# First product of the last expert layer: seven block products in place of eight

## The chip, the cores and the metric

The kernel runs on one core of a Trainium2 chip. A core has TensorE (PE in the profile; PEld is its weight load), VectorE (DVE), ScalarE (ACT), GpSimd (POOL), and SyncE (SP), which issues most transfers. The metric is the device time of one execution in microseconds (us), as the median of several.

## What is computed

```python
x = attn_out.reshape(B * S, D)          # spectral mixing of (4, 3072, 256)
x = _moe_ref(x=x, **moe_kwargs)         # top-1 experts, 384 slots each
...
logits = x @ w_gate                     # last expert layer
P = np.exp(logits - logits.max())
for _ in range(8):                      # Sinkhorn: rows, columns
    ...
for e in range(E):                      # E = 8, D = 256, F = 1024
    h = np.maximum(x @ w1[e], 0.0)
    ye = h @ w2[e]
    out += P[:, e:e + 1] * ye
```

The last layer works on all tokens with every expert. The kernel does it for the 8 x 384 = 3072 slots of the first expert layer; the other rows of the output are zero.

## The kernel before

Every float32 operand of a large product is split into a high part, rounded to what a float32r matmul takes, and a low part, the rest. A product of two such operands is three matmuls that add up in one PSUM bank: high by high, low by high and high by low.

The first expert layer (lines 714 to 739) goes through 8 experts, two halves of the 1024 hidden columns, and four 128-wide tiles each: `mm1` (675) fills a ps_h bank with 6 matmuls of 384 columns, ACT writes the Relu as the high part (682), DVE the low part (683), and `mm2_a` (697), two tiles later, adds it into two ps_yT banks. At an expert's end ACT and DVE write those banks to `x_hi` and `x_lo` (708, 709), the input of the last layer, and `logits2` (685) makes the gate's logits from them, 4 small matmuls for each of 24 tiles of 128 tokens.

The last layer (863 to 910) has blocks of one expert, one half and 512 of the 3072 tokens. For a block PE runs `mm1` for four hidden tiles (24 matmuls of 512 columns, line 680), and then the second product of the block before, `mm2_b` (822): 24 matmuls into two ps_y banks (834). DVE multiplies each bank by the row weights `pb` (843) and adds it to `acc` (844); for expert 1 POOL first multiplies `acc` by expert 0's weights (826). The last expert takes both halves of a block one after the other, its last 512 tokens in two blocks of 256, and `finish` (846) transposes finished tokens and sends each row to its place by an indirect transfer (857).

The order on each engine is the order of the code (`manual_schedule`). PE's products are one block ahead of its second products, so a block's Relus have a whole block's time. The weights of a half come by SP one half ahead (`load_w`, 414, two 512 KB transfers) and are split by ACT and POOL (`split_w`, 426) in four pieces of 512 columns, at blocks 1 to 4 of the half before; three weight sets, w0 to w2, take turns. The Sinkhorn steps (`sink`, 800) are put between the matmuls of the first blocks, each with one small matmul on PE and ten small operations on DVE. ps_h has 3 banks, ps_y and ps_yT share 4.

## Time and profile before

| what | before |
|---|---|
| runs | 1506.34, 1508.4 and 1510.44 us; median 1508.4 |
| the profiled execution's own time | 1509.36 us |
| its span, first to last instruction | 1507.6 us |
| busy in the span | PE 1467.9 (97%), DVE 819.1 (54%), ACT 489.2 (32%), POOL 291.4 (19%) |
| mean granted PE clock | 0.987 |

The page divides the span by engine and by line. A busy PE is not a PE at its peak, since matmuls overlap; the spacing of their starts tells how fast they run. "<-" in a group stands between output and inputs; "idle before" is the time that the engine stood before the group's instructions, with what ended it. The table of stretches gives each engine's busy time within a window, and the granted clock as a share of 2.4 GHz.

### The profile page before, as it was taken

How to read it: one execution, taken by the hardware profiler on the slowest of the kernel's cores; microseconds unless marked ns; L12 is line 12 of the kernel's file. 1: busy time of each engine (PE TensorE's matmuls, PEld its weight loads, DVE VectorE, ACT ScalarE, POOL GpSimd, SP SyncE). 2: the span in 40 equal slices, each digit the busy share in tenths (PEclk: the TensorE clock that was granted, in tenths of full speed). 3: DMA queues.
4: the chain of work that ended last, by engine and by line, in shares of the span. 5: the costliest groups of instructions: out<-in, count | busy, mean ns of one | idle time of the engine just before them, and what ended most of it. 6: DMA issues, size and time to landing. Idle time of an engine off the chain costs nothing.

```text
span 1507.6 us, 19030 instructions
## 1 busy us (share of the span) xinstructions
PE 1467.9 (97%) x7372; PEld 1240.0 (82%) x7372; DVE 819.1 (54%) x1456; ACT 489.2 (32%) x944; POOL 291.4 (19%) x349
## 2 busy tenths in 40 slices
PE   8999897799999999999999999999999999999997
PEld 7988786799988888888888888888888888888887
DVE  4768688465557235545445455455544554454444
ACT  3444565355533222222222222222222222222222
POOL 2344355712211002210100101010000101020222
PEclk9999998899999999999999999999999999999999
DMA  9447771633320411422201010111101011101111
GB/s 243 110 130 177 189 198 45 192 112 112 112 85 1 156 43 56 156 75 91 75 31 57 22 50 28 49 36 42 54 24 49 29 49 28 50 22 28 49 42 37
DMA packets 70601, 118.07 MB, mean 78 GB/s; under 512 B 7334, under 2 KB 41478, under 8 KB 69062
## 3 DMA queue, kind: packets, MB, share of 16 engines
q1 hardware_dynamic: 55078, 94.79, 21.0%
q0 software_dynamic: 14656, 21.71, 5.5%
q8 instruction: 59, 0.97, 0.3%
q10 hardware_dynamic: 768, 0.28, 0.1%
q14 instruction: 40, 0.33, 0.1%
HBM read 88.34 MB, written 28.41 MB: 77 GB/s over the span
## 4 chain that ended last, share of the span: by engine, by line
issue 65%; PE 9%; POOL 6%; DMA 1%; another core or an unknown queue 0%; POOLq 0%; ACT 0%; DVE 0%; SPq 0%; ACTq 0%
POOL w L87 5%; PE ps_h L680 4%; PE ps_yT L704 4%; POOL out_dram L857 1%; POOL acc L826 1%; DMA raw<-in_moe_w_dram 1%; PE lg L689 0%; PE ps_t L668 0%; DMA xg<-xs_d,idx 0%; DMA pb<-p_d 0%; POOLq L87 0%; POOLq L1015 0%; ACT w L86 0%; POOLq L857 0%
## 5 line engine op out<-in xcount | busy, mean ns | idle before, releaser
L682 ACT ACTIVATE hh<-ps_h 128x512 fp32r<-128x512 f32 (+2 forms) x456 | 263.2, 577 | 841.0 <-PE ps_h L680 823.6
L834 PE MATMUL ps_y<-hh,w 128*128 128x512 f32 (+1 forms) x1568 | 499.9, 391 | 0.0
L680 PE MATMUL ps_h<-x_hi,w 128*128 128x512 f32 (+1 forms) x1568 | 493.1, 386 | 0.0
L683 DVE SCALAR_TENSOR_TENSOR hl<-ps_h,hh 128x512 fp32r<-128x512 f32 (+2 forms) x456 | 302.1, 663 | 319.9 <-ACT hh L682 312.6
L834 PEld LDWEIGHTS ps_y<-hh,w 128*128 128x128 f32 x1568 | 292.3, 188 | 66.7
L680 PEld LDWEIGHTS ps_h<-x_hi,w 128*128 128x128 f32 x1568 | 292.6, 188 | 60.2
L834 PE MATMUL ps_y<-hl,w 128*128 128x512 f32 (+1 forms) x784 | 305.6, 390 | 0.0
L680 PE MATMUL ps_h<-x_lo,w 128*128 128x512 f32 (+1 forms) x784 | 302.2, 385 | 0.0
L87 POOL TENSOR_TENSOR w<-raw,w 128x512 fp32r<-128x512 f32 x84 | 109.5, 1305 | 930.6 <-ACT w L86 853.1
L843 DVE TENSOR_TENSOR yp<-ps_y,pb 128x512 f32<-128x512 f32 (+1 forms) x172 | 117.0, 680 | 237.4 <-PE ps_y L834 231.0
L834 PEld LDWEIGHTS ps_y<-hl,w 128*128 128x128 f32 x784 | 147.2, 188 | 33.7
L680 PEld LDWEIGHTS ps_h<-x_lo,w 128*128 128x128 f32 x784 | 147.3, 188 | 29.7
L844 DVE TENSOR_TENSOR acc<-acc,yp 128x512 f32<-128x512 f32 (+1 forms) x172 | 121.6, 707 | 7.4 <-POOL acc L826 1.1
L704 PE MATMUL ps_yT<-hh,w 128*128 128x384 f32 x256 | 77.1, 343 | 4.6 <-issue 2.4
L680 PE MATMUL ps_h<-xgh,w 128*128 128x384 f32 x256 | 78.9, 351 | 0.1
L86 ACT CAST w<-raw 128x512 fp32r<-128x512 f32 x124 | 75.6, 614 | 0.0
L704 PEld LDWEIGHTS ps_yT<-hh,w 128*128 128x128 f32 x256 | 48.2, 191 | 5.3 <-issue 2.8
L680 PEld LDWEIGHTS ps_h<-xgh,w 128*128 128x128 f32 x256 | 48.8, 194 | 0.9 <-ACT xgh L86 0.5
L87 DVE TENSOR_TENSOR ml<-ps_m,mh 128x512 fp32r<-128x512 f32 x48 | 33.2, 692 | 27.7 <-ACT mh L86 27.6
L857 POOL DMA_INDIRECT out_dram<-o,ido x24 | 23.5, 980 | 126.7 <-ACT o L854 121.5
L86 ACT CAST mh<-ps_m 128x512 fp32r<-128x512 f32 x48 | 28.2, 587 | 58.6 <-PE ps_m L158 58.6
L680 PE MATMUL ps_h<-xgl,w 128*128 128x384 f32 x128 | 44.1, 345 | 0.5 <-issue 0.5
(183 smaller groups left out, 1360.0 us busy)
## 6 DMA issues: line engine op xcount, KB each, us to landing
raw<-in_moe_w_dram SPq DMA_DIRECT2D x60, 512.0 KB, 5.4
pb<-p_d SPq DMA_DIRECT2D x88, 256.0 KB, 3.3
out_dram<-zt SPq DMA_DIRECT2D x24, 512.0 KB, 5.4
mf<-in_c_mats_dram POOLq DMA_DIRECT2D x40, 192.0 KB
ds<-d SPq DMA_DIRECT2D x48, 128.0 KB, 3.4
xc<-ds SPq DMA_DIRECT2D x8, 768.0 KB, 6.3
xs_d<-xo SPq DMA_DIRECT2D x32, 192.0 KB, 4.0
xc<-in_x_dram SPq DMA_DIRECT2D x7, 768.0 KB, 13.7
```

The source lines that it names most:

```text
L86: nc.scalar.copy(hi_ap, src)
L87: (lo_engine or nc.vector).tensor_sub(lo_ap, src, hi_ap.bitcast(F32))
L680: nc.tensor.matmul(ps[:, 0:n], l, r[:, h, cols], start=k == 0, stop=k == 5)
L682: nc.scalar.activation(hh, ps[:, 0:n], AF.Relu)
L683: nc.vector.scalar_tensor_tensor(hl, ps[:, 0:n], 0.0, hh.bitcast(F32), op0=ALU.max, op1=ALU.subtract)
L704: nc.tensor.matmul(yT[e][c], l, r, start=fk == 0 and i == 0, stop=fk == 2 * NF - 1 and i == 2)
L826: nc.gpsimd.tensor_mul(acc[:, c, cs], acc[:, c, cs], p0[:, 0:n])
L834: nc.tensor.matmul(ps[:, 0:n], l, r, start=i == 0, stop=i == 3 * NF - 1)
L843: nc.vector.tensor_mul(y[:, 0:n], ps[:, 0:n], pb[:, 0:n])
L844: nc.vector.tensor_add(a, a, y[:, 0:n])
L857: i = nc.gpsimd.indirect_dma_start(out=out, out_offset=bass.IndirectOffsetOnAxis(ap=ido[:, ti % NCH, ti // NCH:ti // NCH + 1], axis=0), in ...
```

## The change

The first product x @ w1[e] is done by Strassen's scheme (in Winograd's form): both operands are cut into two by two blocks, and seven block products stand for eight. On the weight side the blocks are the two 128-row halves of the depth by a pair of 128-wide hidden tiles; on the token side the two depth halves by two token sets, the slots of the even experts of the first layer and those of the odd ones (1536 each). The sums of token blocks, T1 to T4, are made once, at the end of each pair of experts in the first layer (`keep_y`, and two tasks in `later`), and split like x itself. The sums of weight blocks, four 128 by 128 ones for each quarter of the hidden columns, are made by POOL after each load (`sums`), and split by ACT and POOL (`split_r`: 1408 columns a quarter in place of 1024, weights of the second product included).

A unit is one expert, one half, 512 columns of a token set (so 1024 tokens) and one pair of hidden tiles (fp = 0 or 1). It has seven steps. In step i PE runs product i (3 matmuls into a ps_h bank) and 3 or 4 of the 24 second products of the unit before. `post` then makes the four sums of products in the tiles cc: seven additions of a bank and a kept tile on DVE, one copy on ACT, four Relus into the high parts and two in place on ACT, and the low parts, two on POOL and two on DVE. Four ps_y banks (two output halves by two token sets) gather both units of a pair (fp = 0, 1); in the second unit after a pair's start, steps 5 and 6 and the two steps behind them, DVE multiplies each by the row weights and POOL, in the last half DVE, adds it to acc (`evict`). The weight set of the next even quarter is split in a half's third unit, us[2], that of the odd one in the first unit of the next half. hh2 and hl2 of the first layer have 3 buffers in place of 4; the row weights come in one transfer for both token sets; constants move to a pool that ends earlier. The second product's matmuls stay as many. `mm2_b` and the block loop go.

```diff
+    Q = S // 2
+    b_hi = xpl.tile([128, 4, Q], F32R, tag="z1h", name="b_hi")
+    b_lo = xpl.tile([128, 4, Q], F32R, tag="z1l", name="b_lo")
+    t_x = xp.tile([128, 5, Q], F32R, name="t_x")
+    xh = [b_hi[:, i] for i in range(4)] + [t_x[:, i] for i in range(3)]
+    xl = [b_lo[:, i] for i in range(4)] + [t_x[:, 3], t_x[:, 4], wt[0][:, 4608:4608 + Q]]
+    B11, B21, B22, T4, T1, T2, T3 = range(7)
...
+        m, side = divmod(e, 2)
+        terms = ((0, (T1, B11)), (1, (B22,))) if side else ((0, (B11,)), (1, (B21,)))
+        mm = [(h, a[i], w) for h, ops in terms for i in ops for a, w in ((xl, E), (xh, 2 * E))]
...
+    def keep_y(e, y0, y1):
+        m, side = divmod(e, 2)
+        q = slice(cap * m, cap * m + cap)
+        f0, f1 = (xg[:, e].rearrange("p c d -> p (c d)")[:, cap * k:cap * k + cap] for k in range(2))
+        if side == 0:
+            for i, y, f in ((B11, y0, f0), (B21, y1, f1)):
+                split(xh[i][:, q], xl[i][:, q], y)
+                nc.scalar.copy(f, y)
+            return
+        p0, p1_ = (xg[:, e - 1].rearrange("p c d -> p (c d)")[:, cap * k:cap * k + cap] for k in range(2))
+        nc.scalar.copy(f1, y1)
+        nc.vector.tensor_sub(f0, y0, p0)
+        nc.vector.tensor_sub(p0, f1, y0)
+        split(xh[B22][:, q], xl[B22][:, q], y1)
+        nc.gpsimd.tensor_sub(f1, f1, f0)
+        nc.gpsimd.tensor_sub(p1_, p1_, f1)
+        later.append(lambda: (split(xh[T1][:, q], xl[T1][:, q], f0), split(xh[T2][:, q], xl[T2][:, q], f1, nc.gpsimd)))
+        later.append(lambda: (split(xh[T3][:, q], xl[T3][:, q], p0, nc.gpsimd),
+                              split(xh[T4][:, q], xl[T4][:, q], p1_, nc.gpsimd)))
...
-            cs = slice(cap * e, cap * e + cap)
-            for c in range(2):
-                nc.scalar.copy(x_hi[:, c, cs], yT[e][c])
-                nc.vector.tensor_sub(x_lo[:, c, cs], yT[e][c], x_hi[:, c, cs].bitcast(F32))
-            del yT[e]
+            keep_y(e, *yT.pop(e))
...
+    def sums(t, u):
+        a11, a21, a12, a22 = (t[:, 128 * i:128 * i + 128] for i in range(4))
+        s1_, s2_, s3_, s4_ = (u[:, 128 * i:128 * i + 128] for i in range(4))
+        nc.gpsimd.tensor_add(s1_, a21, a22)
+        nc.gpsimd.tensor_sub(s3_, a11, a21)
+        nc.gpsimd.tensor_sub(s2_, s1_, a11)
+        nc.gpsimd.tensor_sub(s4_, a12, s2_)
+
+    WN = 1408
+
+    def split_r(r, t, u, part):
+        w = wt[(1 + r) % 3]
+        for src, o in ((t[:, 0:128], 0), (t[:, 256:512], 128)) if part == 0 else ((u, 384),) if part == 1 else ((t[:, 512:1024], 896),):
+            n = src.shape[1]
+            split(w[:, o:o + n], w[:, WN + o:WN + o + n], src, nc.gpsimd)
...
+    spare = [hp.tile([128, BL], F32R, name=f"h{i}") for i in range(5)]
+    spare += [wt[i][:, o:o + BL] for i, o in ((1, 2816), (1, 3328), (2, 2816), (2, 3328), (0, 2816), (0, 3328), (0, 3840))]
+    pairs = [(spare[2 * i], spare[2 * i + 1]) for i in range(6)]
+    full = [(BL * k, BL) for k in range(Q // BL)]
+    ends = full[:-1] + [(Q - BL, BL // 2), (Q - BL // 2, BL // 2)]
+    units = [(e, h, c0, n, fp) for e in range(E) for h in range(2)
+             for c0, n in (ends if (e, h) == (E - 1, 1) else full) for fp in range(2)]
+    NU2, NS = len(units), 7
...
+    def evict(e, h, c0, n, c, side, ps, last):
+        a = acc[:, c, side, c0:c0 + n]
+        if e == 0 and h == 0:
+            nc.scalar.copy(a, ps[:, 0:n])
+            return
+        y = hp.tile([128, BL], F32, tag="py", name="yp", bufs=2)
+        if e == 0:
+            nc.vector.tensor_add(y[:, 0:n], ps[:, 0:n], a)
+            nc.gpsimd.tensor_mul(a, y[:, 0:n], pbs[0, c0][:, side, 0:n])
+        else:
+            nc.vector.tensor_mul(y[:, 0:n], ps[:, 0:n], pbs[e, c0][:, side, 0:n])
+            (nc.vector if last else nc.gpsimd).tensor_add(a, a, y[:, 0:n])
...
+        seq = [((1, 1), (0, 1), (0, 0), (1, 0)), ((0, 0), (1, 1), (0, 1), (1, 0))][fp]
...
+    PRODS = ((0, B11), (4, T2), (1, B21), (5, T3), (3, T1), (6, B22), (2, T4))
+    MM2 = (3, 4, 3, 4, 3, 4, 3)
...
+            at(us[2], 0, lambda r=r: sums_r(r))
+            for k in range(3):
+                at(us[2], 2 + k, lambda r=r, k=k: split_r(r, rws[r], sus[r], k))
+        r += 1
+        if r < 4 * E:
+            at(us[3], 0, lambda r=r: begin_r(r))
+            at(us[5], 1, lambda r=r: sums_r(r))
+            for k in range(3):
+                at(us[5] + 1, k, lambda r=r, k=k: split_r(r, rws[r], sus[r], k))
...
+    def post(u, i, ps, cc, n, hs):
+        def tile_c():
+            return hp.tile([128, BL], F32, tag="cc", name="cc", bufs=5)
+
+        def high(k, f, side):
+            nonlocal npair
+            hs[f, side] = pairs[npair % 6]
+            npair += 1
+            nc.scalar.activation(hs[f, side][0][:, 0:n], cc[k][:, 0:n], AF.Relu)
+            if k in (0, 3):
+                nc.scalar.activation(cc[k][:, 0:n], cc[k][:, 0:n], AF.Relu)
+
+        def low(k, f, side, eng):
+            hh, hl = hs[f, side]
+            if eng is nc.gpsimd:
+                eng.tensor_sub(hl[:, 0:n], cc[k][:, 0:n], hh[:, 0:n].bitcast(F32))
+            else:
+                eng.scalar_tensor_tensor(hl[:, 0:n], cc[k][:, 0:n], 0.0, hh[:, 0:n].bitcast(F32), op0=ALU.max, op1=ALU.subtract)
+
+        def plus(d, a):
+            nc.vector.tensor_add(cc[d][:, 0:n], ps[:, 0:n], cc[a][:, 0:n])
+
+        if i in (0, 1, 3, 4):
+            cc[(0, 1, None, 2, 3)[i]] = tile_c()
+        if i == 0:
+            nc.scalar.copy(cc[0][:, 0:n], ps[:, 0:n])
+        elif i == 1:
+            plus(1, 0)
+        elif i == 2:
+            plus(0, 0)
+            high(0, 0, 0)
+        elif i == 3:
+            plus(2, 1)
+            low(0, 0, 0, nc.gpsimd)
+        elif i == 4:
+            plus(3, 2)
+            high(3, 1, 1)
+            plus(1, 1)
+        elif i == 5:
+            plus(1, 1)
+            high(1, 0, 1)
+            low(3, 1, 1, nc.gpsimd)
+        else:
+            plus(2, 2)
+            high(2, 1, 0)
+            low(1, 0, 1, nc.vector)
+            at(u + 1, 0, lambda: low(2, 1, 0, nc.vector))
...
+                when = {(0, 1): (u, 5), (1, 1): (u, 6), (0, 0): (u, 7), (1, 0): (u, 8)}
...
+        for i in range(NS):
+            if u < NU2:
+                ai, bi = PRODS[i]
+                ps = ph.tile([128, 512], F32, tag="h", name="ps_h")
+                l_hi, l_lo = w[:, 128 * ai:128 * ai + 128], w[:, WN + 128 * ai:WN + 128 * ai + 128]
+                for k, (l, x_) in enumerate(((l_hi, xh[bi]), (l_hi, xl[bi]), (l_lo, xh[bi]))):
+                    nc.tensor.matmul(ps[:, 0:n], l, x_[:, c0:c0 + n], start=k == 0, stop=k == 2)
+            for _ in range(MM2[i]):
+                fn = next(gen, None)
+                if fn is not None:
+                    fn()
+            if u < NU2:
+                post(u, i, ps, cc, n, hs)
+            run(u, i)
+        prev = (e, h, c0, n, fp, w, hs) if u < NU2 else None
...
```

Three places show the order. On POOL in the last layer, about a half in the middle: before, there were only the four weight pieces of each half (line 87), one per block. Now the third unit of a half reads as follows (zl is a weight set; L750 to L753 the weight sums, L80 low parts of weights, L1020 low parts of the hidden tiles, L934 the additions to acc).

```order
L750 TENSOR_TENSOR su_12440<-rw_12352 128x128
L751 TENSOR_TENSOR su_12440<-rw_12352 128x128
L752 TENSOR_TENSOR su_12440<-su_12440,rw_12352 128x128
L753 TENSOR_TENSOR su_12440<-rw_12352,su_12440 128x128
L80 TENSOR_TENSOR zl_2920<-rw_12352,zl_2920 128x128
L80 TENSOR_TENSOR zl_2920<-rw_12352,zl_2920 128x256
L1020 TENSOR_TENSOR w1_7236<-cc_12438,h4_8958 128x512
L80 TENSOR_TENSOR zl_2920<-su_12440,zl_2920 128x512
L80 TENSOR_TENSOR zl_2920<-rw_12352,zl_2920 128x512
L1020 TENSOR_TENSOR w2_7237<-cc_12490,w1_7236 128x512
L934 TENSOR_TENSOR acc_8953<-acc_8953,yp_12508 128x512
L934 TENSOR_TENSOR acc_8953<-acc_8953,yp_12521 128x512
```

The low part of product 2's sum (first L1020) and that of product 4's (second) stand behind the weights' low parts of their steps.

On DVE, one block of the last layer before:

```order
L683 SCALAR_TENSOR_TENSOR hl<-ps_h,hh 128x512 x4
L843 TENSOR_TENSOR yp<-ps_y,pb 128x512
L844 TENSOR_TENSOR acc<-acc,yp 128x512
L843 TENSOR_TENSOR yp<-ps_y,pb 128x512
L844 TENSOR_TENSOR acc<-acc,yp 128x512
```

And now, the end of an fp = 0 unit (product 4 on) and the start of the next one (cc are the kept sums, L933 the multiplications, L1022 low parts):

```order
L1025 TENSOR_TENSOR cc_11062<-ps_h_11055,cc_11051 128x512
L1025 TENSOR_TENSOR cc_11031<-ps_h_11055,cc_11031 128x512
L1025 TENSOR_TENSOR cc_11031<-ps_h_11067,cc_11031 128x512
L933 TENSOR_TENSOR yp_11078<-ps_y_10927,pb_10964 128x512
L1025 TENSOR_TENSOR cc_11051<-ps_h_11081,cc_11051 128x512
L1022 SCALAR_TENSOR_TENSOR h1_8955<-cc_11031,h0_8954 128x512
L933 TENSOR_TENSOR yp_11091<-ps_y_10944,pb_10964 128x512
L933 TENSOR_TENSOR yp_11104<-ps_y_10972,pb_10964 128x512
L1022 SCALAR_TENSOR_TENSOR h3_8957<-cc_11051,h2_8956 128x512
L1025 TENSOR_TENSOR cc_11117<-ps_h_11108,cc_11102 128x512
L933 TENSOR_TENSOR yp_11124<-ps_y_10984,pb_10964 128x512
```

Each product has a sum of its own; a low part with two SBUF inputs (L1022) stands ahead of the multiplication that clears the second ps_y bank, and one ahead of the next unit's first sum.

On PE, before, the end of one block's second product and the start of the next block's first:

```order
L834 MATMUL ps_y<-hh,w_2920 128x512 x2
L834 MATMUL ps_y<-hl,w_2920 128x512
L834 MATMUL ps_y<-hh,w_2920 128x512
L680 MATMUL ps_h<-x_hi,w_2920 128x512
L680 MATMUL ps_h<-x_lo,w_2920 128x512
L680 MATMUL ps_h<-x_hi,w_2920 128x512 x2
L680 MATMUL ps_h<-x_lo,w_2920 128x512
L680 MATMUL ps_h<-x_hi,w_2920 128x512 x2
```

And now, from the first step of a unit with fp = 1:

```order
L1080 MATMUL ps_h_11459<-b_hi_7328,w1_7236 128x512
L1080 MATMUL ps_h_11459<-b_lo_7329,w1_7236 128x512
L1080 MATMUL ps_h_11459<-b_hi_7328,w1_7236 128x512
L971 MATMUL ps_y_11463<-w1_7236,zl_2920 128x512
L971 MATMUL ps_y_11463<-w2_7237,zl_2920 128x512
L971 MATMUL ps_y_11463<-w1_7236,zl_2920 128x512
L1080 MATMUL ps_h_11476<-t_x_7330,w1_7236 128x512 x3
L971 MATMUL ps_y_11480<-w1_7236,zl_2920 128x512
L971 MATMUL ps_y_11480<-w2_7237,zl_2920 128x512
L971 MATMUL ps_y_11480<-w1_7236,zl_2920 128x512
L971 MATMUL ps_y_11463<-w2_7237,zl_2920 128x512
```

Three matmuls per product alternate with three or four of the second product, whose inputs are in part made in the last steps of the unit before; the second row of its group reads a low part (here in w2).

## Rows read from the trace of the kernel before

**Rows 1.** Busy time by stretch: us, then each engine's busy us, clock, DMA.
```profile
260.00:280.00 20.00, 16.12 (x80) 13.40 (x79) 10.04 (x23) 6.00 (x13) 15.90 (x16) 0.89 0.61 179
...
600.00:1300.00 700.00, 700.00 (x3043) 570.82 (x3042) 352.60 (x507) 171.93 (x293) 65.03 (x50) 1.00 0.16 53
```

**Rows 2.** Timeline of PE: start, us, engine, line, operation, output and inputs.
```profile
431.40 0.17 PE L689 MATMUL lg<-wg2r,x_hi 128*128 128x16 f32 x1
...
432.65 0.49 PE L680 MATMUL ps_h<-x_hi,w 128*128 128x512 f32 x1
...
1001.76 0.39 PE L680 MATMUL ps_h<-x_hi,w 128*128 128x512 f32 x1
...
1007.21 0.40 PE L834 MATMUL ps_y<-hh,w 128*128 128x512 f32 x1
...
1012.80 0.39 PE L680 MATMUL ps_h<-x_hi,w 128*128 128x512 f32 x1
```

**Rows 3.** Groups by form, whole run: count, busy us, mean ns, idle before.
```profile
L680 PE MATMUL ps_h<-x_hi,w 128*128 128x512 f32 x1504 | 481.0, 390 | 0.0
...
L680 PE MATMUL ps_h<-x_lo,w 128*128 128x512 f32 x752 | 293.1, 390 | 0.0
...
L680 PE MATMUL ps_h<-x_hi,w 128*128 128x256 f32 x64 | 12.1, 283 | 0.0
...
L185 POOL TENSOR_TENSOR y<-y,c 128x256 f32<-128x256 f32 x22 | 16.2, 734 | 52.0 <-DVE c L184 48.4 <-ACT z_hi L86 3.6
```

**Rows 4.** Groups by form, 800 to 1300 us.
```profile
L683 DVE SCALAR_TENSOR_TENSOR hl<-ps_h,hh 128x512 fp32r<-128x512 f32 x180 | 124.5, 692 | 116.6 <-ACT hh L682 116.6
...
L682 ACT ACTIVATE hh<-ps_h 128x512 fp32r<-128x512 f32 x180 | 108.0, 600 | 373.9 <-PE ps_h L680 373.9
...
L87 POOL TENSOR_TENSOR w<-raw,w 128x512 fp32r<-128x512 f32 x29 | 37.4, 1290 | 437.6 <-ACT w L86 437.6
```

**Rows 5.** Durations min/median/max ns of three lines; then POOL's and DVE's timeline.
```profile
L843 DVE TENSOR_TENSOR yp<-ps_y,pb x172: 424/693/693, 579.4 to 1499.1; 128x512 f32<-128x512 f32 x164, 128x256 f32<-128x256 f32 x8
...
L844 DVE TENSOR_TENSOR acc<-acc,yp x172: 424/693/1764, 580.4 to 1499.6; 128x512 f32<-128x512 f32 x164, 128x256 f32<-128x256 f32 x8
...
L87 POOL TENSOR_TENSOR w<-raw,w x84: 1282/1290/1751, 319.4 to 1352.3; 128x512 fp32r<-128x512 f32 x84
...
601.12 2.55 POOL L826 TENSOR_TENSOR acc<-acc,pb 128x512 f32<-128x512 f32 x2
...
602.45 1.76 DVE L844 TENSOR_TENSOR acc<-acc,yp 128x512 f32<-128x512 f32 x1 [0.28 <-POOL acc L826]
```

**Rows 6.** Timeline: a bank's last matmul (and the next one), its Relu, its low part.
```profile
1002.90 0.61 PE L680 MATMUL ps_h<-x_hi,w 128*128 128x512 f32 x2
...
1003.33 0.60 ACT L682 ACTIVATE hh<-ps_h 128x512 fp32r<-128x512 f32 x1 [5.86 <-PE ps_h L680]
...
1003.96 0.69 DVE L683 SCALAR_TENSOR_TENSOR hl<-ps_h,hh 128x512 fp32r<-128x512 f32 x1 [0.59 <-ACT hh L682]
```

**Rows 7.** Timeline: clearing the two ps_yT banks of expert 7.
```profile
428.34 1.00 ACT L708 CAST x_hi<-ps_yT 128x384 fp32r<-128x384 f32 x2 [1.64 <-PE ps_yT L704]
...
428.86 1.08 DVE L709 TENSOR_TENSOR x_lo<-ps_yT,x_hi 128x384 fp32r<-128x384 f32 x2 [2.07 <-ACT x_hi L708]
```

**Rows 8.** Timeline of DVE: first and last of a Sinkhorn step's ten operations.
```profile
447.53 0.17 DVE L783 TENSOR_SCALAR rc<-ps_s 128x8 f32<-128x8 f32 x1 [2.39 <-PE ps_s L781]
...
450.49 0.17 DVE L776 SCALAR_TENSOR_TENSOR cs<-pr,cs 128x8 f32<-128x8 f32 x1
```

**Rows 9.** Timeline of the end: last matmul, last two output transfers.
```profile
1498.79 0.28 PE L834 MATMUL ps_y<-hh,w 128*128 128x256 f32 x1
...
1501.54 0.97 POOL L857 DMA_INDIRECT out_dram<-o,ido  x1 [4.97 <-ACT o L854]
...
1502.82 0.98 POOL L857 DMA_INDIRECT out_dram<-o,ido  x1 [0.30 <-issue]
```

More of the change, by code (lines that the diff above doesn't have):

```diff
@@ L685, in logits2 @@
+        nc.vector.scalar_tensor_tensor(hl, ps[:, 0:cap], 0.0, hh.bitcast(F32), op0=ALU.max, op1=ALU.subtract)
     def logits2(e):
[L686 to L692 removed]
+        m, side = divmod(e, 2)
@@ new lines, in finish @@
+    def finish(c0, side, g):
+        pt = ph.tile([128, 2, D], F32, tag="h", name="ps_o")
+        o = hp.tile([128, BL], F32, tag="py", name="o", bufs=2)
+        k0 = c0 // 128 + 2 * g
+        for t in range(2):
+            for c in range(2):
+                nc.tensor.transpose(pt[:, t, 128 * c:128 * c + 128], acc[:, c, side, 128 * (k0 + t):128 * (k0 + t) + 128], ident)
+        nc.scalar.copy(o, pt.rearrange("p t d -> p (t d)"))
+        for t in range(2):
+            m, c = divmod(k0 + t, NCH)
+            e = 2 * m + side
+            i = nc.gpsimd.indirect_dma_start(
+                out=out, out_offset=bass.IndirectOffsetOnAxis(ap=ido[:, c, e:e + 1], axis=0),
+                in_=o[:, D * t:D * t + D], in_offset=None, bounds_check=N - 1, oob_is_err=False)
+            tc.declare_no_dep(i.ins, group="rows", reason="each slot has a row of its own")
+            tc.add_to_no_dep_group("rows", i.ins)
@@ L913, in _split12 @@
+    while tasks:
+        run(*min(tasks))
 def _split12(a):
```

270 lines of the change are left out of this document (141 added, 129 removed).

## Prediction

> **What bounds the kernel now.** I read the busy table by stretches first. In the last expert layer (600 to 1300 us) PE is busy 700.00 of 700.00 us at a granted clock of 1.00, that is 2.4 GHz, while DVE has 352.60, ACT 171.93 and POOL 65.03 [rows 1]. So PE bounds it, and each matmul taken out is worth its spacing, as long as the three others deliver in time.
>
> The spacing comes from the timeline, not from the mean durations, which overlap. One block has 24 first products from 1001.76 to 1007.21 and 24 second products from 1007.21 to 1012.80: 0.227 and 0.233 us each [rows 2]. The groups by form count the first products: 1504 + 752 on 512 columns, and a 64 + 32 on 256 (the 32 stand in the same ratio as the 752 to the 1504) [rows 3].
>
> **What the change removes.** A unit (256 hidden columns by 1024 tokens) has seven products of 3 matmuls where 24 stood, and the same 24 second products. There are 94 full units and 4 of half width: 282 full matmuls and 12 half ones go, 282 x 0.227 + 12 x 0.114 = **65.4 us**. A unit becomes 21 x 0.227 + 24 x 0.233 = 10.36 us; before, 11.05. The pace of the mixed stream isn't in the trace: all at 0.227 would give 94 x 24 x 0.006 = 14 us more, all at 0.233 would take 94 x 21 x 0.006 = 12 us; I keep the two paces where they are, and both ends for the range. The Trainium skill (TensorE: Matmul & The Clock Gate, Back-to-back issue gap) puts an isolated matmul at full clock at N/2.4 + 2.5 ns, 215.8 ns for 512 columns; by that estimate the gain would be 62.2 us, and the row's 227 ns decides.
>
> **What it adds beside PE.** Per unit DVE gets 7 sums of a PSUM bank with a kept tile, 2 low parts and (mean) 2 multiplications: 11 operations of 0.69 us [rows 4, 5], 7.6 of 10.36 us. ACT gets 1 copy, 4 Relus, 2 Relus in place: 7 x 0.60 = 4.2 us [rows 4], and casts of weights. POOL gets 2 low parts and (mean) 2 additions to acc at 1.29 [rows 4], 5.2 us, and a third of a weight set: four 128-wide sums and 1408 columns of low parts, about 4 x 0.4 + 3.6 = 5.2 us by the 734 ns of a 256-wide one [rows 3], so 1.7. POOL is at 6.9 of 10.36. No engine reaches PE on the mean, so the extra work is hidden wherever results are early enough. What counts is the order in which they come.
>
> **Two kinds of DVE operation.** Multiplications that read PSUM and one SBUF tile stay at 693 ns at most; additions that read two SBUF tiles reach 1764 [rows 5]. The one at 602.45 started while POOL was in the second of two additions (601.12, 2.55 in all) and ended 0.69 after POOL did [rows 5]. So of the new operations the 7 sums and the multiplications run free, and the 2 low parts on DVE wait for a POOL operation in progress; POOL's own reach 1751 instead of 1290 [rows 5].
>
> **The hand-over from an fp = 0 unit to the next.** I set the queues against PE's 10.36 us with these durations, from the unit's first matmul. Products start at 0, 1.38, 2.99, 4.37, 5.98, 7.36 and 8.97; ACT starts 0.43 after the start of a bank's last matmul (1002.90 to 1003.33) and DVE 0.03 after ACT [rows 6], so a product is read 0.89 after its own start.
> - Plain case. Product 4 is read at 6.87, DVE's sum ends at 7.56, the two Relus near 8.7, POOL's low part runs 8.8 to 10.1. PE wants it as the second matmul of the next unit's second product, at 10.35 + 0.69 + 0.23 = 11.27: early by 1.2. POOL then adds (10.0 to 11.3). DVE's low part is ready to start at 9.86 + 0.69 = 10.55, is held to 11.3, ends at 12.0, and the multiplication behind it, which frees a ps_y bank, at 12.6. PE wants that bank at 10.35 + 1.38 + 0.69 = 12.42. PE stands about 0.25 us.
> - With a weight split in that unit (third unit of a half, us[2]). The casts stand behind product 2's Relus on ACT, so POOL starts the low parts near 5.9; 128, 256, low part of product 2, 512, 512 take 0.4 + 0.7 + 3 x 1.26 = 4.9 (two in a row take 2.55, so 1.26 more for each that follows), to 10.7. The low part that PE wants at 11.27 ends at 12.0, or, if DVE's waiting low part goes first, at 12.7: PE stands 0.7 to 1.4 us. I take 1.0.
> - fp = 1 to fp = 0: the next unit begins with second products whose parts are 2 us old. Nothing.
>
> There are 45 hand-overs with multiplications: 14 with a split (14 x 1.0), 31 plain (31 x 0.25): **22 us**. Bounds: 0, if DVE or POOL run a little ahead of this, and 80, if each POOL operation takes the 1.75 of the row (below).
>
> **The other terms.** (1) Router logits: twelve 128-token tiles take 6 matmuls instead of 4; 12 took 1.25 us (431.40 to 432.65) [rows 2], so 24 x 0.104 = 2.5 us, on PE's path. (2) keep_y: a pair of ps_yT banks was cleared by two ACT and two DVE operations, 428.34 to 429.94 [rows 7]; now it takes four ACT ones or three chained DVE ones, about 0.35 us later, and the next expert's second product wants the bank: 7 x 0.35 = 2.5 us (0 to 7). POOL's two subtractions per pair and the low parts of T2 to T4 have a whole expert's time. hh2 with 3 buffers instead of 4: the third is free before it is written; nothing. (3) First unit: no second products cover it, and the logits of expert 7 wait for T1, which comes through ACT and DVE behind keep_y: 3 us (1 to 6). (4) Sinkhorn: one step of columns and rows takes DVE 447.53 to 450.66, 3.1 us [rows 8]. Units 2 to 4 hold two steps each: 9 operations of 0.69 and 6.2 make 12.4 against 10.36: 3 x 2.0 = 6 us (2 to 9). The units before and after hold one step or none. (5) Last half: additions on DVE and half-width units, chains of the same length in half the time: 2 us (1 to 5). (6) End: PE's last matmul is at 1498.79 and two output transfers are issued at 1501.54 and 1502.82, 1.28 apart [rows 9]. Now four banks are cleared after it (8 half-width DVE operations, 3.1 us), and four transfers follow from about 4.6 on: the last starts near 8.4 instead of 3.9 behind the last matmul, **4.5 us** more. (7) Loads: weights come in quarters with the same bytes, the row weights as 46 transfers for 88 of half the size; SP waits for none of the new work for longer than a unit, and they are a unit ahead: nothing.
>
> Sum against the profiled execution's own 1509.4: 1509.4 - 65.4 + 2.5 + 2.5 + 3 + 6 + 22 + 2 + 4.5 = 1486.5. The median of the runs, 1508.4, is 1.0 lower: **1485.5 us**. Forecast: faster.
>
> **The rivals.**
> - Hidden: the hand-overs cost nothing, and the terms (2) to (6) are near their low ends (1, 2, 2, 1, 3.5; with (1) 12 in all): 1509.4 - 65.4 + 12 - 1 = 1455. For it: each engine has a quarter of its time free, and three ps_h banks take up two products of delay. Against it: the split puts five POOL operations ahead of one that PE needs, whatever the mean.
> - POOL holds up PE (slower). If POOL's 512-wide operations take 1.75 as in the row where they met DVE, the plain hand-over becomes: low part to 10.5, addition to 12.2, DVE's low part to 12.9, bank at 13.5, 1.1 us late; with a split POOL reaches that low part at 12.5 or 13.2, and it is 3.3 late. 31 x 1.1 + 14 x 3.3 = 80: 1509.4 - 65.4 + 20.5 + 80 - 1 = 1543.5. It decides from a mean of (65.4 - 20.5) / 45 = 1.0 us per hand-over; my forecast has 0.49. For it: POOL goes from a tenth to two thirds, and meets two DVE low parts per unit. Against it: 1290 is the median and 1751 the extreme [rows 5].
> - The clock falls. Where PE was busy 16.12 of 20.00 us the granted clock was 0.89, a mix of its two levels of 1.2 and 2.4 GHz [rows 1]. At that clock the matmuls of the stage, 94 x 10.36 + 4 x 5.2 = 995 us, would take 12% longer: near 1608. Against it: the stops forecast here are about a microsecond in 20, and PE is at 95% or more. The Trainium skill (same page, A second HAM failure mode: psum-queue depth-cycling) describes matmul groups that cycle through PSUM banks with short stops making the clock swing; no run here shows that at this share of stops.
> - Nothing measurable (within 0.3%, 4.5 us, about what a measurement of this kernel can tell): the stops of PE eat the gain almost exactly.
> - That the change does less than it says is ruled out: the order shows three matmuls per product.
>
> **How the numbers follow.** Forecast 0.50 (its own range 1468 to 1502: 14 us of pace and some of the hand-overs either way), hidden 0.24, POOL 0.17, clock 0.03, no difference 0.06. Faster 0.50 + 0.24 = 0.74, within 0.3% 0.06, slower 0.17 + 0.03 = 0.20. For 8 times in 10 the range takes in hidden with some of the faster pace (1450) and the first part of the POOL case up to a mean near 1.1 us per hand-over and the slower pace's half (1518); the rest of that case and the clock are left out.
>
> **What would show it.** Right: 2058 first products; PE's idle time in the stage near 22 us, released by POOL (low part) in the third unit of each half and by DVE (multiplication) in the other fp = 0 units; DVE near 75% and POOL near 65% busy; low parts on DVE over 0.69 and sums at 0.69; last matmul some 13 us before the end instead of 8.7. Wrong: a pace of 0.24 or more between matmuls with nothing waited for, a granted clock under 0.98 in the stage, or PE waiting for ps_h banks in every unit, which would make DVE the bound.

## The result and the profile after

| kernel | median of the runs, us | runs | profiled execution, us |
|---|---|---|---|
| before | 1508.3 | 1506.3 to 1510.4 | 1509.4 |
| changed | 1528.5 | 1521.6 to 1535.2 | 1521.6 |

The ratio is 1.0133 (95% interval 1.0086 to 1.0181): slower, where 1485.5 was forecast with a range of 1450 to 1518. The profiled execution of the changed kernel is the fastest of its four, 7 us under their median, and what makes that difference no trace here shows. From the start of the first "first product" to the start of the last "second product" (called the stage below) the kernel before takes 1070.1 us and the changed one 1078.5 (427.8 to 1506.3). The 65 us of matmuls did go; about 74 came back in the stage.

The busy table of the changed kernel by stretches (us, then each engine's busy us with its instructions, PE's clock, DMA) answers [rows 1]. Three parts of the stage are shown: its first units, its middle and its last units.

```profile
400.00:440.00 40.00, 38.50 (x211) 36.42 (x211) 19.02 (x33) 20.34 (x43) 25.16 (x29) 0.91 0.24 79
440.00:500.00 60.00, 48.96 (x202) 38.36 (x201) 49.35 (x109) 23.47 (x44) 18.83 (x21) 0.93 0.00 1
600.00:1300.00 700.00, 680.33 (x2926) 546.06 (x2925) 508.10 (x716) 314.95 (x543) 476.63 (x433) 1.00 0.17 53
1420.00:1505.00 85.00, 72.81 (x395) 61.40 (x394) 54.96 (x98) 32.39 (x65) 43.72 (x41) 0.96 0.15 50
```

PE was busy 700.00 of 700.00 us before. Now it stands 20 us of those 700, though DVE is at 73% and POOL at 68%: no engine is full, PE waits for single results. In the first units it stands 11 of 60 us and the clock is 0.93, in the last ones 12 of 85 at 0.96. What it waits for, over the whole stage (us in total, times, longest):

```profile
PE ps_y L971 <- POOL w L1020: 19.4, 14, 1.4
PE ps_y L971 <- ACT acc L926: 9.5, 2, 5.6
PE ps_h L1080 <- ACT o L943: 6.1, 3, 3.2
PE ps_y L971 <- POOL zl L1020: 3.5, 1, 3.5
PE ps_h L1080 <- DVE cc L1025: 3.4, 5, 1.1
PE ps_y L971 <- DVE yp L933: 3.3, 13, 0.3
```

The first and last of these rows recur in every half (six units) of the middle; the second belongs to the first units, the third and fourth to the last.

**The middle.** The timeline of POOL and of PE where a half's third unit hands over to its fourth (start, duration, operation, idle time before it and its releaser):

```profile
667.88 1.31 POOL L1020 TENSOR_TENSOR w<-cc,h 128x512 fp32r<-128x512 f32 x1
669.13 1.31 POOL L80 TENSOR_TENSOR zl<-su,zl 128x512 fp32r<-128x512 f32 x1
670.39 1.30 POOL L80 TENSOR_TENSOR zl<-rw,zl 128x512 fp32r<-128x512 f32 x1
671.65 1.73 POOL L1020 TENSOR_TENSOR w<-cc,w 128x512 fp32r<-128x512 f32 x1
```

```profile
671.64 0.40 PE L971 MATMUL ps_y<-w 128*128 128x512 f32 x1
673.43 0.51 PE L971 MATMUL ps_y<-w,w 128*128 128x512 f32 x1 [1.39 <-POOL w L1020]
```

Two 512-wide operations of the weight split (L80) stand between the two low parts (L1020) on POOL; the second low part ends at 673.38, and the second matmul of the unit's second product starts 1.79 us after the first instead of 0.23. That stop stands 14 times, 64.6 us apart. A smaller one (0.65 instead of 0.23 between two starts) stands where the first unit hands over: DVE's low part of 1.71 us, from 649.84 to 651.55 beside an addition on POOL (0.69 when POOL is idle), holds up the multiplication that frees the bank.

```profile
649.84 1.71 DVE L1022 SCALAR_TENSOR_TENSOR w<-cc,h 128x512 fp32r<-128x512 f32 x1
```

```profile
652.20 1.19 PE L971 MATMUL ps_y<-h,w 128*128 128x512 f32 x4 [0.26 <-DVE yp L933]
```

The fifth unit hands over with a third stop of the same kind (0.54 between two starts, at 695.62). Such short stops are easily missed: since a matmul counts as busy for 0.39 us, a start 0.54 after the last leaves only 0.15 of idle time.

**The first units.** DVE, ACT and PE around the longest stop:

```profile
461.11 0.16 DVE L854 TENSOR_SCALAR rc<-ps_s 128x8 f32<-128x8 f32 x1
...
462.02 1.42 DVE L857 TENSOR_TENSOR pr<-pr,rc 128x200 f32<-128x200 f32 x1
...
467.07 1.27 DVE L1025 TENSOR_TENSOR cc<-ps_h,cc 128x512 f32<-128x512 f32 x2
```

```profile
467.78 0.63 ACT L1013 ACTIVATE w<-cc 128x512 fp32r<-128x512 f32 x1 [4.53 <-DVE cc L1025]
468.32 0.57 ACT L926 COPY acc<-ps_y 128x512 f32<-128x512 f32 x1
```

```profile
468.94 0.79 PE L971 MATMUL ps_y<-w 128*128 128x512 f32 x1 [5.58 <-ACT acc L926]
```

A chain of four: a Sinkhorn step (461.11 to 467.1) holds DVE's sum at 467.07, that sum holds a Relu on ACT, the copy of a ps_y bank stands behind the Relu on ACT, and PE wants that bank. The step takes 6.0 us where 3.1 was read [rows 8]: POOL is at work without a pause beside it, from 460.80 to 467.1, with the weight split and low parts, of which this is one.

```profile
463.17 1.39 POOL L80 TENSOR_TENSOR zl<-su,zl 128x512 fp32r<-128x512 f32 x1
```

The other stop of the row for ACT acc, 3.9 us before 498.41, has the same chain; its step takes 4.3 us (492.27 to 496.55), with low parts and weight sums on POOL beside it, but no weight split.

**The last units.** ACT's copies of output rows and PE, then POOL and PE some 17 us later:

```profile
1480.87 0.59 ACT L943 COPY o<-ps_o 128x512 f32<-128x512 f32 x1 [2.64 <-DMA out_dram<-o,ido]
1485.16 0.59 ACT L943 COPY o<-ps_o 128x512 f32<-128x512 f32 x1 [3.39 <-DMA out_dram<-o,ido]
```

```profile
1485.80 0.58 PE L1080 MATMUL ps_h<-b_hi,w 128*128 128x256 f32 x1 [3.19 <-ACT o L943]
...
1503.69 0.86 PE L971 MATMUL ps_y<-zl,w 128*128 128x256 f32 x5 [3.45 <-POOL zl L1020]
```

```profile
1501.90 0.98 POOL L947 DMA_INDIRECT out_dram<-o,ido  x1 [0.30 <-issue]
1502.89 0.74 POOL L1020 TENSOR_TENSOR zl<-cc,zl 128x256 fp32r<-128x256 f32 x1
```

The output rows' tile `o` shares a ring of two buffers with the multiplied sums `yp` (tag "py" in `finish` and `evict`); before, it had three of its own. ACT waits for the scatter that empties a buffer, Relus stand behind that copy, and `ps_o` itself holds one of the three ps_h banks (before, one of the four that ps_y uses). Later a low part stands behind four scatter issues, about 1.0 us each and 0.3 apart.

### The profile page after: what moved, and what is told of

Same layout as the page of the kernel before. It is cut to its first block, busy times and chain, and to the rows that moved or that the text cites. A ratio compares the mean times of both kernels' runs of the same rounds, so it can differ in the third digit from the quotient of the medians.

```text
span 1519.8 us, 20338 instructions
## 1 busy us (share of the span) xinstructions
PE 1428.5 (94%) x7102; PEld 1192.4 (78%) x7102; DVE 1061.7 (70%) x1796; ACT 698.6 (46%) x1326; POOL 888.9 (58%) x915
## 4 chain that ended last, share of the span: by engine, by line
PE 59%; DVE 10%; POOL 8%; issue 3%; ACT 2%; DMA 1%; POOLq 0%; ACTq 0%; DVEq 0%
PE ps_y L971 27%; PE ps_h L1080 24%; PE ps_h L686 4%; PE ps_yT L735 3%; DVE cc L1025 3%; POOL w L1020 3%; POOL w L80 3%; DVE w L1022 2%; DVE h L1022 1%; DVE yp L933 1%; POOL zl L80 1%; PE lg L700 1%; ACT h L1013 1%; ACT cc L1015 1%; POOL out_dram L947 0%
## 5 line engine op out<-in xcount | busy, mean ns | idle before, releaser
L1025 DVE TENSOR_TENSOR cc<-ps_h,cc 128x512 f32<-128x512 f32 (+1 forms) x686 | 451.1, 676 | 252.7 <-PE ps_h L1080 238.3
L1013 ACT ACTIVATE h<-cc 128x512 fp32r<-128x512 f32 (+1 forms) x197 | 122.9, 624 | 335.7 <-DVE cc L1025 333.6
L934 POOL TENSOR_TENSOR acc<-acc,yp 128x512 f32<-128x512 f32 x156 | 217.8, 1410 | 35.1 <-DVE yp L933 31.9
L971 PE MATMUL ps_y<-h,w 128*128 128x512 f32 (+1 forms) x732 | 216.8, 389 | 2.6 <-DVE yp L933 2.3
L1080 PE MATMUL ps_h<-b_hi,w 128*128 128x512 f32 (+1 forms) x544 | 212.2, 392 | 4.6 <-ACT o L943 4.6
L1080 PE MATMUL ps_h<-t_x,w 128*128 128x512 f32 (+1 forms) x544 | 169.0, 393 | 4.9 <-DVE cc L1025 3.4
L971 PEld LDWEIGHTS ps_y<-h,w 128*128 128x128 f32 x732 | 134.8, 189 | 35.7 <-DVE yp L933 6.2
L933 DVE TENSOR_TENSOR yp<-ps_y,pb 128x512 f32<-128x512 f32 (+1 forms) x172 | 112.6, 666 | 29.1 <-POOL acc L934 23.4
L1015 ACT ACTIVATE cc<-cc 128x512 f32<-128x512 f32 (+1 forms) x196 | 122.4, 625 | 6.3
L971 PE MATMUL ps_y<-zl,w 128*128 128x512 f32 (+1 forms) x360 | 113.0, 390 | 8.7 <-ACT acc L926 3.9
L1020 POOL TENSOR_TENSOR zl<-cc,w 128x512 fp32r<-128x512 f32 (+1 forms) x33 | 41.6, 1260 | 119.9 <-ACT cc L1015 110.1
L1020 POOL TENSOR_TENSOR h<-cc,h 128x512 fp32r<-128x512 f32 (+1 forms) x66 | 84.2, 1288 | 43.7 <-ACT cc L1015 31.6
L1080 PE MATMUL ps_h<-b_lo,w 128*128 128x512 f32 (+1 forms) x272 | 105.9, 389 | 0.0
L80 POOL TENSOR_TENSOR w<-rw,w 128x128 fp32r<-128x128 f32 (+2 forms) x60 | 49.4, 839 | 74.6 <-ACT w L79 74.6
```

The lines of the kernel that those rows point to most:

```text
L80: (lo_engine or nc.vector).tensor_sub(lo_ap, src, hi_ap.bitcast(F32))
L933: nc.vector.tensor_mul(y[:, 0:n], ps[:, 0:n], pbs[e, c0][:, side, 0:n])
L934: (nc.vector if last else nc.gpsimd).tensor_add(a, a, y[:, 0:n])
L971: yield lambda l=l, r=r, c=c, side=side, st=st, sp_=fp == 1 and k == final[side] and i == 2: nc.tensor.matmul(banks[c, side][:, 0:n], l, r ...
L1013: nc.scalar.activation(hs[f, side][0][:, 0:n], cc[k][:, 0:n], AF.Relu)
L1015: nc.scalar.activation(cc[k][:, 0:n], cc[k][:, 0:n], AF.Relu)
```

## The experiments

**Theory.** The loss has three places with causes of their own: POOL's order in the third unit and DVE's in the first (middle), Sinkhorn steps on DVE with bank copies behind Relus on ACT (first units), `o` buffers and then scatter issues ahead of a low part (last units). **Rivals.** POOL or DVE is simply too full, so that a repair moves the stop; half-width units are too short; the clock is low for a reason that isn't the stops. Ratios below are to the kernel before on the same chip; the changed kernel stands at 1.0133.

### 1. The split a unit later

```diff
-            at(us[2], 0, lambda r=r: sums_r(r))
+            at(us[3], 5, lambda r=r: sums_r(r))
             for k in range(3):
-                at(us[2], 2 + k, lambda r=r, k=k: split_r(r, rws[r], sus[r], k))
+                at(us[3], 6 + k, lambda r=r, k=k: split_r(r, rws[r], sus[r], k))
```

> Edit: the sums and the split of the even weight quarter of a half move from the third unit, where four additions of evicted sums pass POOL, to the fourth unit's last slots and the fifth's first; those weights are needed only in the next half. Theory (hand-over in a full POOL): the stop of 1.78 us that PE makes once in a half, waiting for POOL w L1020, goes in all 14 halves that have it; 14 x 1.55 us = 22 us less, about 1506 us against a median of 1528.5; the second stop of the half (0.65 us) stays. Rival (POOL is full everywhere, so work put elsewhere only moves the stop): a stop of like length appears in the fourth or fifth unit and the time stays within 5 us of 1528. Start and end of the stage read as in the changed kernel under both.

Measured: 1.0000 (0.9983 to 1.0017), stage 1061.2 us. The 14 stops of 1.79 us are gone and none of that length came up in the fourth or fifth unit. What is left are three small ones in each half, one per hand-over (0.64, 0.50 and 0.55 us between two starts); the third unit's stands where the long one was. The middle, and what PE waits for between 550 and 1400 us:

```profile
600.00:1300.00 700.00, 694.27 (x2985) 557.20 (x2984) 525.27 (x731) 322.34 (x552) 483.25 (x442) 1.00 0.17 55
```

```profile
PE ps_y L971 <- DVE yp L933: 5.2, 25, 0.3
```

### 2. The second bank a slot earlier

```diff
-                when = {(0, 1): (u, 5), (1, 1): (u, 6), (0, 0): (u, 7), (1, 0): (u, 8)}
+                when = {(0, 1): (u, 5), (1, 1): (u, 5), (0, 0): (u, 7), (1, 0): (u, 8)}
```

> Edit: the second bank of a pair's first token set is multiplied one slot earlier, ahead of the low part that DVE computes in the last slot. Theory (that multiplication comes late because it stands behind a low part that POOL's lock stretches): the 13 stops of 0.65 us, PE waiting for DVE yp L933, go and the 1.78 us stops stay; 6 to 10 us less, about 1520 us. Rival (DVE is late by its whole load, not by this order): the stop moves to the sum that is now behind the multiplication, and the time stays within 3 us of 1528.

Measured: 1.0033 (1.0019 to 1.0047), stage 1062.6 us: more than expected. A half lost 1.0 us (64.6 to 63.6, worked out under 3), so more than the one stop of 0.65 between two starts: the fifth unit's of 0.54 went with it, for the same reason. Those for POOL w stay, and are all that is left between 550 and 1400 us.

```profile
600.00:1300.00 700.00, 684.78 (x2970) 556.44 (x2970) 502.06 (x726) 316.68 (x551) 493.08 (x441) 1.00 0.17 55
```

```profile
PE ps_y L971 <- POOL w L1020: 17.9, 13, 1.4
```

### 3. Both

> Edit: the edits of the first two experiments together (even quarter's sums and split in the fourth and fifth unit, second bank multiplied one slot earlier). The first took the stage from 1078.5 to 1061.2 us, the second to 1062.6. Theory (two stops with causes of their own, a full POOL and an order on DVE): the gains add, a half falls from 64.6 to 62.2 to 62.5 us, its pace without stops, and the stage to about 1045 us: 33 us under the changed kernel, ratio to the kernel before about 0.991. Rival (both only give POOL and DVE the same slack once): the stage stays at 1058 us or above, ratio 0.998 or more.

Measured: 0.9873 (0.9845 to 0.9900), stage 1041.6 us.

```profile
600.00:1300.00 700.00, 700.00 (x3052) 572.26 (x3051) 521.07 (x747) 325.99 (x562) 504.59 (x448) 1.00 0.18 56
```

PE doesn't stand any more in the middle. A half has 270 matmuls, so 2926 in 700 us are 64.6 us a half, 3052 are 61.9; 62.2 was worked out for PE without stops. POOL and DVE do more per us than before the repair, and hold nothing up. The rival of a full engine falls: two edits of order, which take no operation away, give 2.6% (1.0133 to 0.9873) and make the change 1.3% faster than the kernel before, clear of the interval. The first units gain almost nothing by it: the first seven take 92.9 us, 93.2 in the changed kernel. Their first long stop shrinks with the split gone from beside it (the Sinkhorn step takes 3.9 us, 465.83 to 469.73), but it doesn't go:

```profile
471.58 0.50 PE L971 MATMUL ps_y<-w 128*128 128x512 f32 x1 [3.50 <-ACT acc L926]
```

### 4. Sinkhorn steps further apart, all low parts on POOL there

```diff
-        at(1 + (k + 1) // 2, 4 if k % 2 == 0 else 1, fn)
+        at(1, 4 + (9 * k) // 2, fn)
...
-            if k in (0, 3):
+            if k in (0, 3) or 1 <= u <= 7:
...
-            low(1, 0, 1, nc.vector)
-            at(u + 1, 0, lambda: low(2, 1, 0, nc.vector))
+            eng = nc.gpsimd if 1 <= u <= 7 else nc.vector
+            low(1, 0, 1, eng)
+            at(u + 1, 0, lambda: low(2, 1, 0, eng))
```

> Edit: the Sinkhorn steps go 4.5 slots apart instead of 3.5, over units 1 to 7, the first load of the gate values one unit later, and in units 1 to 7 all four low parts are POOL's. Theory (DVE is overfull there, and ACT's copies of the first banks stand behind Relus that wait for DVE): the stops of 5.98 and 4.30 us at 463 and 494 us go or fall under 1 us, the granted clock of 440 to 500 us rises from 0.93 to 0.97 or more; 15 to 25 us less, about 1508 us. Rival (the stops come of the weight copies and eviction copies on ACT, whatever DVE does): stops of over 3 us stay and the time is within 5 us of 1528. Rival (the clock is low there for another reason): the stops go and the clock stays at 0.93; 12 us less.

Measured: 1.0111 (1.0087 to 1.0134), stage 1081.5 us: a miss. The longest stop falls from 5.6 to 3.4 us, but others come up, and the clock of 440 to 500 us is 0.89. With low parts or the weight split on POOL beside them single Sinkhorn operations are still up to four times as long as with POOL idle (L857 1.41, 1.33 and 1.34 us in three of eight steps, 0.37 in the others). The edit also gives ACT, which is in the chain, two more Relus in place per unit (second hunk), so it doesn't test the distance between the steps alone:

```profile
PE ps_y L971 <- ACT acc L926: 5.4, 3, 3.4
PE ps_h L1081 <- DVE cc L1025: 3.8, 4, 2.3
PE ps_y L971 <- POOL w L1020: 1.6, 1, 1.6
```

### 5. Two Sinkhorn iterations

```diff
-ITERS = 8
+ITERS = 2
```

> Edit: 2 Sinkhorn iterations instead of 8; six are left out of the computation. Theory (Sinkhorn steps on DVE make the stops of the first half): the two long stops (5.98, 4.30 us) and the smaller ones after 450 us go, the granted clock of 440 to 500 us is 0.97 or more, and 18 to 26 us of the changed kernel's time go: ratio to the kernel before about 0.999. Rival (weight copies and bank copies on ACT make them): at least one stop of over 3 us stays though no Sinkhorn step is near it, ratio 1.008 or more.

Measured: 1.0039 (1.0016 to 1.0062), stage 1066.7 us. Without six of the steps some 14 us go by the ratio, 11.8 by the stage: less than expected, yet no stop of over 3 us is left in the first units. One place keeps its stops, next to the steps that are left (471 to 475 us), half by ACT's copies and half by POOL, on which the weight split stands there; from there to 535 us PE waits for nothing:

```profile
PE ps_y L971 <- ACT acc L926: 1.9, 1, 1.9
PE ps_y L971 <- POOL w L1020: 1.8, 1, 1.8
```

### 6. Sinkhorn steps cut in two

```diff
-    sink = [lambda: (sink_exp(), sink_rows())] + [lambda k=k: sink_cols(k == ITERS - 1) for k in range(ITERS)]
+    sink = [sink_exp, sink_rows]
+    for k in range(ITERS):
+        sink.append(lambda: sink_b(state["cs"]))
+        if k < ITERS - 1:
+            sink.append(sink_rows)
...
-        at(1 + (k + 1) // 2, 4 if k % 2 == 0 else 1, fn)
+        at(1, 4 + (40 * k) // 17, fn)
```

> Edit: each Sinkhorn step is cut in two (columns, rows) and the 18 pieces go every 2.35 slots over units 1 to 7; the first load of the gate values one unit later. Theory A (a whole step of 3 to 5 us in one slot lets the three banks of the first product run full): no stop of over 1.5 us is left between 440 and 510 us, 12 to 18 us less, ratio about 1.004. Theory B (DVE has more to do in these units than they last, however it is cut): PE's idle time there falls by no more than the one unit that the pieces gain, 3 to 6 us, stops of over 2 us stay, ratio about 1.010.

Measured: 1.0059 (1.0033 to 1.0084), stage 1071.3 us. Between the two theories: the stops of 5.6 and 4 us are gone with the same work on DVE, and PE is busy 56.58 of the 60 us from 440 to 500 (48.96 before the edit), but part of it comes back after 500 us, and a wait for the steps themselves (cs) is new:

```profile
PE ps_s L852 <- DVE cs L847: 3.1, 3, 1.5
PE ps_y L975 <- ACT acc L930: 1.8, 3, 0.6
```

So cut into halves the same work makes no long stop, which points to the size of the piece that DVE takes in one go. The halves also reach over more units than the steps did; that this alone isn't enough is argued from experiment 4, where whole steps went as far apart and stops of 3.4 us stayed, but which gave ACT more to do as well. What the remaining 4.9 us come of isn't shown.

### 7. Buffers for the output rows

```diff
-        o = hp.tile([128, BL], F32, tag="py", name="o", bufs=2)
+        if not obuf:
+            for _ in range(2):
+                t = hp.tile([128, 1024], F32, tag="rw", name="o", bufs=2)
+                obuf.extend((t[:, 0:512], t[:, 512:1024]))
+            obuf.append(hp.tile([128, 512], F32, tag="su", name="o"))
+        o = obuf[no[0] % 5]
+        no[0] += 1
```

> Edit: the output rows of a finish are copied into five buffers of their own (where the weight quarters were), no longer into two that they share with the multiplied sums. Theory (in the last half ACT's copy waits for the scatter DMA to release its buffer, and the Relus and the bank that PE needs stand behind it): the stops of 1.77 and 3.47 us at 1480 and 1482 us and most of those between 1452 and 1474 go; the last 80 us lose 4 to 9 us, with the clock that follows them up to 12; about 1519 us. Rival (the half-width units are too short for four transposes and a copy in each three-bank ring): PE keeps its waits for ps_h banks and the time stays within 3 us of 1528.

Measured: 1.0083 (1.0062 to 1.0104), stage 1074.8 us. 3.7 us of the stage, where 4 to 9 were expected: ACT waits for no scatter any more, and PE not for `o`, but new waits for POOL take most of it back (1430 to 1500 us):

```profile
PE ps_y L979 <- POOL zl L1028: 4.2, 2, 3.2
PE ps_y L979 <- POOL h L1028: 2.8, 2, 2.2
PE ps_y L979 <- POOL w L1028: 1.7, 1, 1.7
```

They are low parts behind scatter issues, as in the last group shown of the changed kernel.

### 8. Buffers, and the last low parts on DVE

```diff
-            if eng is nc.gpsimd:
+            if eng is nc.gpsimd and u < NU2 - 6:
```

> Edit: five buffers of their own for the output rows, as before, and in the last six units all low parts on DVE, so that none stands behind a scatter issue on POOL. Theory (with the buffers apart, what is late next is a low part behind POOL's scatter issues of 1 us each): the stops of 1.9, 2.5 and 3.5 us before the end go, the idle time of PE after 1440 us falls from about 13 to 4 us; 14 us under the changed kernel, ratio to the kernel before about 1.004. Rival (the half-width units are too short for DVE, which then carries low parts, multiplications and additions): stops of like length for DVE, ratio 1.008 as without this edit, or above.

Measured: 1.0088 (1.0056 to 1.0120), stage 1073.2 us: a miss, no better than 7. The low parts wait for no issue, but DVE has them all and PE waits for DVE (1440 to 1520 us). In 2.4 us of PE's waits here the profile names no releaser; what they are stays open.

```profile
PE ps_h L1088 <- issue: 2.4, 3, 1.8
PE ps_h L1088 <- DVE cc L1033: 2.3, 3, 1.0
PE ps_y L979 <- DVE yp L933: 2.1, 4, 1.0
```

The miss is in part the clock's. PE stands less than in 7, 7.6 of the stage's last 85 us against 10.5, but the clock of these 85 us is 0.96 against 0.98: right behind the longest of these stops (1.8 us, to 1489.20) it is 0.59, mostly the lower of its two levels (1.2 and 2.4 GHz):

```profile
1490.00:1498.00 8.00, 6.48 (x31) 5.66 (x30) 6.81 (x19) 1.97 (x6) 0.15 (x1) 0.59 0.05 16
```

### 9. Buffers, and the finishes two at a time

The edit of 7, and low parts on POOL as in the changed kernel:

```diff
-                    at(u + 1, (3 if u < NU2 else 0) + k, lambda
+                    at(u + 1, ((6, 7, 13, 14) if pn == BL else (6, 8))[k] if u < NU2 else k, lambda
```

> Edit: five buffers of their own for the output rows, low parts on POOL as in the changed kernel, and the finishes of a pair put into the last slot of a unit and the first of the next, so that no more than two scatter issues stand ahead of a low part. Theory (two causes in a row: ACT's copy waiting for a buffer, then low parts behind scatter issues on POOL): PE's idle time after 1440 us falls from about 13 to 5 us or less, no stop of over 1.5 us is left before the last second product, ratio to the kernel before 1.005 to 1.007. Rival (short units, whatever is moved): stops of 2 to 4 us come up elsewhere as in the two experiments on the end before, ratio 1.008 or more.

Measured: 1.0017 (1.0003 to 1.0031), stage 1063.3 us, 15.1 less than the changed kernel. The last 85 us of the stage:

```profile
1400.00:1485.00 85.00, 82.94 (x460) 70.84 (x459) 66.62 (x114) 39.70 (x78) 51.95 (x51) 1.00 0.16 50
```

PE is busy 82.94 of 85 us, where the changed kernel had 72.81, with the same half-width units and the same number of scatters: the rival of the short units falls. The clock is 1.00 instead of 0.96 once the stops are gone. What the new order does without the buffers was not run.

### 10. All together

The edits of 1, 2, 6 and 9; each column step three slots behind its row step, and the logits two slots later.

> Edit: the edits on the steady units, the half Sinkhorn steps (each column step now three slots behind its row step, since PE waited for cs), the logits two slots later (PE waited for t_x), and the end as in the experiment beside this one. Theory (three places with causes of their own, so gains add): from a ratio of 1.013, 0.025 for the steady units, 0.008 to 0.010 for the start and 0.005 to 0.008 for the end: 0.970 to 0.976, stage about 1027 us against 1078.5, no stop of over 1.5 us in it. Rival (the stops of start and end are one reserve that only moves): no better than the two steady edits alone, 0.987 within 0.003.

Measured: 0.9696 (0.9675 to 0.9718), 1453.6 us against 1499.0 for the kernel before on that chip; stage 1015.2 us. The gains of 3, 6 and 9 (0.0260, 0.0074, 0.0116) add up to 0.0450, and 1.0133 - 0.0450 is 0.9683; the 1.0133 has an interval of 0.005 either way, so this sum is good to about a per cent. The stage says the same more closely: 36.9, 7.2 and 15.1 us make 59.2, and it lost 63.2. The 4 us beyond the sum lie in the first units, where this kernel also changes the distance of the half steps and the place of the logits: the first nine take 101.4 us here, 106.3 in 6 and 113.9 in the changed kernel. The three places have causes of their own: a common reserve of slack would have given less than the sum.

```profile
PE 1403.8 (97%) x7102; PEld 1186.3 (82%) x7102; DVE 1053.5 (73%) x1796; ACT 698.5 (48%) x1326; POOL 903.3 (62%) x915
```

```profile
440.00:500.00 60.00, 57.56 (x248) 45.89 (x247) 53.41 (x120) 28.87 (x53) 24.99 (x27) 0.97 0.03 10
400.00:440.00 40.00, 38.51 (x215) 35.56 (x215) 21.87 (x39) 22.04 (x46) 24.00 (x28) 1.00 0.24 79
```

The longest wait left in the stage is 1.5 us, for a first sum on DVE. Every instruction of the changed kernel is there, as many on each engine; what differs is when it is put into its queue, and five buffers.

## Why the prediction was wrong

- **What is taken out: right.** 2058 first products are left. In experiment 3, where PE has no stops in the middle, a half takes 61.9 us against 62.2 by the two paces of [rows 2]; the mixed stream's pace needed no allowance.
- **The logits, (1): right.** 24 more matmuls at 0.11 us are 2.6 us, against 2.5. Only a quarter of them, 0.6 us, lies in the stage.
- **No engine full: right, and not enough.** DVE 73% and POOL 68% in the middle (forecast 75 and 65); sums of a bank with a kept tile 676 ns in the mean; low parts on DVE from 0.69 to 1.75 us, as POOL happened to be at work.
- **Hand-overs, 22 us: the place and the mechanism right, the size too small.** Behind the split, 1.79 - 0.23 = 1.56 us are lost each of 14 times, and 0.1 more at the next start, where 0.7 to 1.4 was worked out and 1.0 taken: DVE's waiting low part went first, the later of the two cases. A plain hand-over loses 0.42 us in the first unit of a half and 0.31 in the fifth, with 0.1 behind each, so about 0.5 where 0.25 was worked out. In the first unit the odd quarter's split stands on POOL ahead of the low parts (641.19 to 647.2), which the step left out; in the fifth nothing does. The step also misread its row: the addition of [rows 5] ended at 604.21, 0.54 after POOL's operation at 603.67 (a multiplication, L826) and not 0.69, and so do the low parts here (651.55 against 651.00); by that reading the plain case would have come out smaller still. Stage 1078.5 less 1041.6 is 37 us for both, or 0.82 per hand-over. The POOL rival's mechanism is the one seen, but not its premise (POOL's 512-wide operations have a median of 1.30 us, not 1.75; the low part that PE waits for takes 1.73), and 0.82 is under the 1.0 from which it decides. With 37 in place of 22 the sum gives 1501.5 against 1509.4: by hand-overs alone the change would have been faster.
- **First units, (3) and (4), 9 us: this step failed.** The step's 3.1 us came from a row in which POOL was idle; with the weight split beside it, it is 6.0. It counted two Sinkhorn steps in units 2 to 4, and unit 5 holds two as well; the long stops are in units 3 and 5. And the sum counted what DVE has to do, not who stands behind it: the bank copies on ACT behind Relus that wait for DVE were no term. Those two stops alone cost 9.5 us; PE stands 11 us from 440 to 500, and the clock of 0.93 comes on top. Experiment 3 tells the two parts of the cause from each other: with the split moved away the step takes 3.9 us, and the stop is still 3.5, so the order of the queues makes the stop and POOL lengthens it. The wait of the logits for T1 was foreseen in (3): 1.5 us (DVE 1.2, ACT 0.3).
- **Last half, (5), 2 us: this step failed too.** It looked at chains of operations, not at buffers: that `o` went from a ring of three to two shared with `yp` stands in the diff and had no price, nor had scatter issues ahead of low parts on POOL. Experiment 9 gets 15 us back.
- **The end, (6): right.** 13.5 us from the last second product to the end of the span, 8.8 before: 4.8 against 4.5.
- **keep_y, (2): too dear.** The stage begins at 427.8 us, 0.9 earlier than before, but that says nothing of keep_y: the changed kernel and the experiments have the same code up to there and begin it anywhere from 418.3 to 435.5 us. From the first expert's logits to the stage it is 123.1 us before (305.57 to 428.67) and 125.8 now (302.07 to 427.82); 18 logit matmuls make 2.0 of the 2.7, which leaves 0.7 where 2.5 was priced. Where PE stops there (three times 0.5 us, which the sum shows only in part), it waits for low parts of weights on POOL and not for the ps_yT banks.
- **The clock: nothing in the middle, something at both ends.** The middle keeps 1.00 with stops of 1.6, 0.4 and 0.3 us every 64.6, and the rival's 1608 is far off. The rows of 0.91, 0.93 and 0.96 cost up to 11 us (an estimate: 9% of 40, 7% of 60 and 4% of 85 us), for which the forecast had no term; in the last units the clock is back at 1.00 once the stops are gone (experiment 9), in the first ones at 0.97 to 1.00 (experiment 10). The Trainium skill (TensorE: Matmul & The Clock Gate, A second HAM failure mode: psum-queue depth-cycling) describes matmul groups that cycle through PSUM banks with short stops making the clock swing; the middle, whose row stays at 1.00, shows no such swing at its share of stops.

The stage was to be 1038.3 us (1070.1 - 65.4 + 0.6 + 3 + 6 + 22 + 2) and took 1078.5. Of the 40 us, about 15 are hand-overs (37 against 22), 13 the last units (15 against 2); the remaining 12 stand in the first units. That remainder agrees with their own time: the first seven units take 93.2 us (427.82 to 521.02), where their matmuls make 69 by the paces of [rows 2], 21 x 0.227 for the first unit, 6 x 10.36 for the others and 2 for the logits. So some 22 to 24 us are lost there, against 9.6 in the forecast. Experiment 6 mends 7 to 8 of them, experiment 10 some 12 (first nine units 113.9, 106.3 and 101.4 us); of the rest the cause stays open.
